# One activation-table set for the first group's decays and norms, in a kernel that TensorE bounds later on

## The chip, the cores and the metric

One core of one Trainium2 chip. The metric is the device time of one launch in microseconds (us). A run is compared with runs of the kernel before on the same chip in the same job. The program uses one core, and each run also lists the mean clock that was granted to TensorE. In the profiles PE is TensorE (matmuls), ACT is ScalarE (functions such as Exp), DVE is VectorE, POOL is GpSimd, and SP is SyncE, which issues nearly all of the loads here. A half clock means that the granted clock is 0.50.

## The reference, cut to what matters

Four sequences of 5824 tokens with 256 channels go through a gated recurrence; its result goes through two up-projections (256 to 1024), their product, and two more matrices that the kernel folds into one (1024 to 256).

```python
sig_r = 1.0 / (1.0 + np.exp(-r_gate))
sig_i = 1.0 / (1.0 + np.exp(-i_gate))
log_a = c * sig_r * np.log(np.clip(a_base, 1e-06, 1.0 - 1e-06))[None, None, :]
a_t = np.exp(log_a)                                    # decay
norm = np.sqrt(np.maximum(1.0 - a_t * a_t, 1e-06))     # norm
x_gated = norm * sig_i * x
h = a_t[:, t] * h + x_gated[:, t]                      # for each t
...
a = x @ w1; b = x @ w2
h = a * b @ w3
return (h @ w_out).astype(np.float32)
```

## The kernel before

The tokens are cut into 46 chunks, and the chunks into 17 groups. In Python, a small model of the engines gives each job a time, and the jobs are emitted in the order of these times, so each engine's program order is fixed. Between some of ACT's functions the traces show a table load, an instruction of its own (1283 ns in the mean in before). A job carries a `kind`: the table set that the model thinks it needs (0: tanh and exp, 1: square root, 2: exp and log). Only group 0 (chunks 0 to 2) makes its norm with Ln and Exp; the other groups use Sqrt.

```python
def decay(c, cb):
    ...
    nc.scalar.activation(out=a, in_=pr, func=AF.Exp, scale=la4[:, cb:cb + 1], bias=la4[:, cb:cb + 1])

def root(c):
    w = sizes[c]
    if any(c in g for g in groups[:N_LOG]):            # N_LOG = 1
        n = T["n", c][:, :, :w]
        nc.scalar.activation(out=n, in_=n, func=AF.Ln, scale=-1.0, bias=1.0)
        nc.scalar.activation(out=n, in_=n, func=AF.Exp, scale=0.5)
        return
    ...                                                # Sqrt

def up(c, mp, nm, w_sb):                               # the up-projections on PE
    pp = psum.tile([P, 2, CT], F32, name=nm, tag="pab")
    for _ in range(warm.get((nm, c, mp), 0)):          # warming matmuls, overwritten afterwards
        nc.tensor.matmul(out=pp[:, 0, :P], lhsT=ident, rhs=ident, start=True, stop=True)
    ...

def rates():
    nc.scalar.preload_act_table_set("natural_log_exp_and_others")
    nc.scalar.activation(out=la4, in_=la4, func=AF.Exp, scale=-1.0)
    nc.scalar.activation(out=la4, in_=la4, func=AF.Ln, bias=1.0)
    ...

# ... the model gives `order`; w3 comes in eight pieces, loaded through two buffers (wf),
# cast by DVE (w_t), transposed by PE (ptw), copied by DVE (w3t), multiplied by PE (pw)
for _, _, key in sorted(order):
    if jobs[key]["fn"]:
        jobs[key]["fn"]()
```

Of the kernel before, what the change touches and what calls it, by code (L numbers as in the profile page):

```python
# [20 lines left out]
def kernel(  # L21
# [12 lines left out]
    nc = tc.nc  # L34
# [47 lines left out]
    T = {}  # L82
# [8 lines left out]
    DV_COPY = set()  # L91
# [214 lines left out]
    def copy_to(dve, dst, src_ps):  # L306
        if dve:
            nc.vector.tensor_copy(out=dst, in_=src_ps)
        else:
            nc.scalar.copy(out=dst, in_=src_ps)  # L310

    def copy(c, mp):
        w = sizes[c]
        sa = ffn.tile([P, 2, CT], BF16, name="sa", tag="sa")
        copy_to(mp == 0 and c in DV_COPY, sa[:, :, :w], T["pa", c, mp][:, :, :w])
        T["sa", c, mp] = sa

    def product(c, mp):
# [84 lines left out]
        nc.vector.tensor_copy(out=ident, in_=ident_f)  # L403

    def rates():
        nc.scalar.preload_act_table_set("natural_log_exp_and_others")
        nc.scalar.activation(out=la4, in_=la4, func=AF.Exp, scale=-1.0)
        nc.scalar.activation(out=la4, in_=la4, func=AF.Ln, bias=1.0)
        nc.vector.tensor_scalar(la4, la4, -1.0, LN_LO, op0=ALU.mult, op1=ALU.max)
        nc.vector.tensor_scalar(la4, la4, LN_HI, 4.0, op0=ALU.min, op1=ALU.mult)  # L410
# [10 lines left out]
    jobs = {}  # L421
# [4 lines left out]
    def job(key, eng, occ, lat, due, fn, after=(), new=None, uses=(), dma=0.0, kind=None, lock=0):  # L426
        due += OFFSET.get(key[0], 0.0) + SHIFT.get(key[:2], 0.0)
        jobs[key] = dict(eng=eng, occ=occ, lat=lat, due=due, fn=fn, after=list(after), new=new, dma=dma, kind=kind,
                         lock=lock, bulk=dma > 0 and key[0] not in ("turn_r", "turn_u", "store", "fold_t"))
        for u in uses:  # L430
            users.setdefault(u, []).append(key)
# [3 lines left out]

    job(("ident",), "DVE", 0.3, 0.35, -1.0, cast_ident)
    job(("la",), "ACT", 0.42, 1.0, 0.0, rates, [("tanh_i", 0)], kind=2)

    def weight(key, piece, dst, due, new=None):
# [33 lines left out]
    for k, g in enumerate(groups):  # L473
        log = k < N_LOG
        for c in g:
# [50 lines left out]
            for mp in range(4):  # L526
                t = U + SLOT / 4 * mp * f
                w = 0.8635 * f * (1.7 if c == 0 else 1)
                job(("pa", c, mp), "PE", w, w + 0.22, t, partial(up, c, mp, "pa", w1_sb),
                    [("cast", c), ("w1", mp // 2)], ("pab", ("pa", c, mp)), [("y", c)])  # L530
                job(("pb", c, mp), "PE", w, w + 0.27, t + 0.01, partial(up, c, mp, "pb", w2_sb),
                    [("pa", c, mp), ("w2", mp // 2)], ("pab", ("pb", c, mp)), [("y", c)])
                e, o, s = ("DVE", 0.065, 1.067) if mp == 0 and c in DV_COPY else ("ACT", 0.05, 0.853)
                job(("copy", c, mp), e, o + s * f, o + s * f + (0.115 if e == "DVE" else 0.15), t + 0.9, partial(copy, c, mp),
                    [("pa", c, mp)], ("sa", ("sa", c, mp)), [("pa", c, mp)])
                job(("product", c, mp), "DVE", 0.065 + 1.067 * f, 0.18 + 1.067 * f, t + 2.0, partial(product, c, mp),
                    [("copy", c, mp), ("pb", c, mp)] + ([("product", c, mp - 1)] if mp else []),
                    None if mp else ("g", ("g", c)), [("sa", c, mp), ("pb", c, mp)])
            for j in range(sizes[c] // P):
# [5 lines left out]
                if c == len(sizes) - 1:  # L545
                    e, o, l = ("ACT", 0.265, 0.42) if j % 2 else ("DVE", 0.332, 0.467)
# [4 lines left out]
                elif j % 2:  # L551
                    e, o, l = ("DVE", 0.599, 0.734) if c in DV_EVAC else ("ACT", 0.48, 0.63)
# [21 lines left out]
    def startable(key, t):  # L574
        b = jobs[key]
        for d in b["after"]:
            if d not in done:
                return False
            if (done[d][0] if jobs[d]["eng"] == b["eng"] and not jobs[d]["dma"] else done[d][1]) > t:
                return False  # L580
        if b["new"]:
            pool = b["new"][0]
            if len(taken[pool]) >= BUFS[pool]:
                for u in users[taken[pool][-BUFS[pool]]]:
                    if u not in done or done[u][1] > t:
                        return False
        if b["lock"] and port_free > t:
            return False
        if b["kind"] is not None and in_run is not None and run_of.get(key) != in_run:
            return False  # L590
        return not b["bulk"] or dma_free <= t + BACKLOG

    events = [0.7, 0.75]
    while any(waiting.values()):
# [3 lines left out]
        for e in engines:  # L598
            if free[e] > t:
                continue  # L600
            key = next((k for k in waiting[e][:80] if startable(k, t)), None)
# [33 lines left out]

    nc.scalar.dma_start(out=la4, in_=a_param.rearrange("(cb p) -> p cb", p=P))

    for _, _, key in sorted(order):
        if jobs[key]["fn"]:
            jobs[key]["fn"]()  # L640
# [1 line left out]
_INS = ['x', 'r_gate', 'i_gate', 'a_param', 'moe_w1', 'moe_w2', 'moe_w3', 'moe_w_out']  # L642
_OUTS = [((23296, 256), 'float32')]
# [25 lines left out]
```

## Time and profile before

| | before |
|---|---|
| time, the first three runs | 532.75 to 534.76 us, median 534.08 |
| the profiled run | 531.5 us (span of the core 529.7), mean granted clock 0.997 |
| busy: PE, ACT, DVE, POOL | 94%, 89%, 84%, 65% of the span |
| table loads | 38, each 1283 ns |

The busy shares are an average over a start of some 70 us, in which nearly every engine waits for another in turn, and a long stretch in which PE is full. The prediction below shows the stages.

### The profile page before, as it was taken

The page shows a single profiled execution, that of the slowest core. Times are in us where ns is not written, and L with a number is a line of the kernel's source. Part 1 is how long each engine was busy: PE and PEld are TensorE (multiplying, and loading weights), DVE is VectorE, ACT ScalarE, POOL GpSimd, SP SyncE. Part 2 cuts the span into 40 slices and gives each one's busy share as a digit, 9 for nine tenths or more (in the row PEclk, how much of TensorE's full clock was granted, in tenths as well). Part 3 has the DMA queues.
Part 4 walks back from the last instruction along what each step waited for, and adds up shares of the span by engine and source line. Part 5 has one row for each costly group of instructions (what it writes and reads, how often), then busy time and mean ns, then how long its engine had stood idle before and what let it go on. Part 6 is the DMA issues. An engine that isn't in the chain of part 4 may idle for free.

```text
span 529.7 us, 8819 instructions
## 1 busy us (share of the span) xinstructions
PE 499.7 (94%) x3199; PEld 308.1 (58%) x3199; DVE 445.0 (84%) x373; ACT 473.4 (89%) x556; POOL 343.6 (65%) x266
## 2 busy tenths in 40 slices
PE   1569889999999999999999999999999999999997
PEld 0456566555666565656656566665556566556556
DVE  0679987999988888988899988989988889899842
ACT  6999999999899998989989999899989999995552
POOL 3347787577758666788675787787685757875100
PEclk9989999999999999999999999999999999999999
DMA  8999959999998999999599797979999988534113
GB/s 304 399 340 325 303 161 263 323 261 267 324 285 209 266 245 265 237 217 274 160 276 278 201 281 178 277 203 252 260 262 237 268 238 244 125 81 101 40 54 106
DMA packets 178828, 124.32 MB, mean 235 GB/s; under 512 B 88672, under 2 KB 174432, under 8 KB 178784
## 3 DMA queue, kind: packets, MB, share of 16 engines
q1 hardware_dynamic: 178512, 123.76, 85.3%
q8 instruction: 25, 0.41, 0.3%
q14 instruction: 19, 0.16, 0.1%
q10 hardware_dynamic: 272, 0.00, 0.0%
HBM read 78.91 MB, written 23.86 MB: 194 GB/s over the span
## 4 chain that ended last, share of the span: by engine, by line
PE 82%; DVE 6%; DMA 4%; ACT 4%; issue 2%; POOL 1%; DVEq 0%; ACTq 0%; POOLq 0%
PE po L333 27%; PE pa L302 27%; PE pb L302 27%; DVE g_t L322 2%; DVE h_t L283 2%; DMA r_t<-in_r_gate_dram 2%; DMA rt<-th_r 1%; DMA ut<-u_t 1%; DVE nrm L268 1%; PE pw L398 1%; ACT L255 1%; POOL u_t L212 1%; DMA la<-in_a_param_dram 1%; ACT a_t L241 1%; DVE w_t L370 1%
## 5 line engine op out<-in xcount | busy, mean ns | idle before, releaser
L322 DVE TENSOR_TENSOR g_t<-sa,pb 128x1024 bf16<-128x1024 bf16 (+1 forms) x184 | 219.0, 1199 | 54.3 <-ACT sa L310 39.2
L302 PEld LDWEIGHTS <-w_sb 128*128 128x128 bf16 x1472 | 143.9, 98 | 143.6 <-issue 3.5
L310 ACT CAST sa<-pa 128x1024 bf16<-128x1024 f32 (+1 forms) x184 | 183.0, 998 | 28.5 <-PE pa L302 26.7
L302 PE MATMUL pb<-y_t,w_sb 128*128 128x512 bf16 (+1 forms) x736 | 187.8, 378 | 1.5 <-DVE g_t L322 1.2
L302 PE MATMUL pa<-y_t,w_sb 128*128 128x512 bf16 (+1 forms) x736 | 187.5, 377 | 0.9 <-DVE g_t L322 0.9
L333 PE MATMUL po<-wp_sb,g_t 128*128 128x256 bf16 x1456 | 180.7, 273 | 0.5 <-ACT wp_sb L414 0.5
L333 PEld LDWEIGHTS <-g_t 128*128 128x128 bf16 x1456 | 142.5, 98 | 45.3 <-issue 0.6
L283 DVE TENSOR_TENSOR_SCAN h_t<-a_t,h_t,nrm 128x512 f32<-128x512 f32 (+3 forms) x90 | 135.0, 1509 | 1.8
L248 POOL TENSOR_TENSOR nrm<-a_t 128x512 f32<-128x512 f32 x80 | 97.4, 1231 | 45.0 <-ACT a_t L241 42.3
L212 POOL TENSOR_TENSOR u_t<-th_i,x_t 128x512 bf16<-128x512 f32 x80 | 121.3, 1532 | 5.0 <-issue 2.8
L291 POOL CAST y_t<-h_t 128x1024 bf16<-128x1024 f32 (+1 forms) x42 | 48.6, 1158 | 68.7 <-DVE h_t L283 57.5
L196 POOL TENSOR_SCALAR th_i<-th_i 128x1024 f32<-128x1024 f32 x44 | 59.5, 1353 | 26.3 <-ACT th_i L191 26.3
L310 ACT COPY ot<-po 128x512 f32<-128x512 f32 (+1 forms) x91 | 53.0, 583 | 17.5 <-PE po L333 16.1
L241 ACT ACTIVATE a_t<-rt,la 128x512 f32<-128x512 bf16 x80 | 63.4, 816 | 2.0 <-DMA rt<-th_r 1.9
L268 DVE SCALAR_TENSOR_TENSOR nrm<-nrm,ut 128x1024 f32<-128x1024 f32 x40 | 60.8, 1521 | 1.6 <-ACT nrm L257 1.1
L191 ACT ACTIVATE th_i<-i_t 128x1024 f32<-128x1024 f32 (+1 forms) x46 | 48.4, 1054 | 2.3 <-DMA i_t<-in_i_gate_dram 2.2
L257 ACT ACTIVATE nrm<-nrm 128x1024 f32<-128x1024 f32 x43 | 44.9, 1063 | 0.2
L184 ACT ACTIVATE th_r<-r_t 128x1024 bf16<-128x1024 f32 x40 | 42.3, 1065 | 0.0
L220 PE MATMUL ptr<-ident,th_r 128*128 128x128 bf16 x44 | 4.5, 260 | 17.0 <-ACT th_r L182 15.7
L257 ACT ACT_TABLE_LOAD x15 | 19.2, 1283 | 0.3
L248 DVE TENSOR_TENSOR nrm<-a_t 128x512 f32<-128x512 f32 (+1 forms) x12 | 12.1, 1053 | 6.4 <-ACT a_t L241 6.4
L220 PEld LDWEIGHTS <-th_r 128*128 128x128 bf16 x44 | 3.5, 116 | 17.9 <-ACT th_r L182 16.9
(39 smaller groups left out, 148.8 us busy)
## 6 DMA issues: line engine op xcount, KB each, us to landing
i_t<-in_i_gate_dram SPq DMA_DIRECT2D x45, 512.0 KB, 5.4
x_t<-in_x_dram SPq DMA_DIRECT2D x45, 512.0 KB, 4.8
r_t<-in_r_gate_dram SPq DMA_DIRECT2D x45, 512.0 KB, 5.4
out_dram<-ot SPq DMA_DIRECT2D x89, 256.0 KB, 3.6
wf<-in_moe_w_dram SPq DMA_DIRECT2D x12, 512.0 KB, 5.2
wf<-in_moe_w_out_dram SPq DMA_DIRECT2D x2, 512.0 KB, 6.9
rt<-th_r SPq DMA_TRANSPOSE x40, 4.9
ut<-u_t SPq DMA_TRANSPOSE x40, 4.8
```

Of the source, the lines that this page charges most:

```text
L196: nc.gpsimd.tensor_scalar(t, t, 1.0, 1.0, op0=ALU.add, op1=ALU.mult)
L212: nc.gpsimd.tensor_mul(out=u.rearrange("p cb j q -> p j cb q")[:, js], in0=cut(t)[:, js], in1=cut(T["x", c])[:, js])
L241: nc.scalar.activation(out=a, in_=pr, func=AF.Exp, scale=la4[:, cb:cb + 1], bias=la4[:, cb:cb + 1])
L248: eng.tensor_mul(out=T["n", c][:, cb, :w], in0=T["a", c][:, cb, :w], in1=T["a", c][:, cb, :w])
L257: nc.scalar.activation(out=T["n", c][:, :, :w], in_=T["n", c][:, :, :w], func=AF.Sqrt, scale=-1.0, bias=1.0)
L268: nc.vector.scalar_tensor_tensor(out=T["n", c][:, :, :w], in0=T["n", c][:, :, :w], scalar=1e-3, in1=T["pu", c][:, :, :w], op0=ALU.max, op1 ...
L283: nc.vector.tensor_tensor_scan(T["h", c][:, cb, lo:hi], T["a", c][:, cb, lo:hi], T["n", c][:, cb, lo:hi], init, ALU.mult, ALU.add)
L291: eng.tensor_copy(out=T["y", c][:, :, :w], in_=T["h", c][:, :, :w])
L302: nc.tensor.matmul(out=pp[:, q, :w], lhsT=w_sb[:, cb, m * P:(m + 1) * P], rhs=T["y", c][:, cb, :w], start=(cb == 0), stop=(cb == NCB - 1))
L310: nc.scalar.copy(out=dst, in_=src_ps)
L322: nc.vector.tensor_mul(out=T["g", c][:, 2 * mp:2 * mp + 2, :w], in0=T["sa", c, mp][:, :, :w], in1=T["pb", c, mp][:, :, :w])
L333: nc.tensor.matmul(out=po, lhsT=T["g", c][:, k, j * P:(j + 1) * P], rhs=wp_sb[:, k, :], start=(k == 0), stop=(k == KD - 1), skip_group_che ...
```

## The change

The intent: have one table set active from the first decay of group 0 to its last norm, where the compiler had put in a load in front of every Ln and every Exp (six loads, the first at 17.25 us, the last at 28.24, 1.28 us each).

```diff
@@ rates
-        nc.scalar.preload_act_table_set("natural_log_exp_and_others")
         nc.scalar.activation(out=la4, in_=la4, func=AF.Exp, scale=-1.0)
@@ end of the program
+    table = None
     for _, _, key in sorted(order):
-        if jobs[key]["fn"]:
-            jobs[key]["fn"]()
+        kind = jobs[key]["kind"]
+        if kind == 2 and table != 2:
+            nc.scalar.preload_act_table_set("natural_log_exp_and_others")
+        if kind is not None:
+            table = kind
+        jobs[key]["fn"]()
```

Two lines more turn `mp == 0 and c in DV_COPY` into `(c, mp) in DV_COPY`; the set is empty in both, so they change nothing.

More of the change, by code (lines that the diff above doesn't have):

```diff
@@ L314, in copy @@
         sa = ffn.tile([P, 2, CT], BF16, name="sa", tag="sa")
-        copy_to(mp == 0 and c in DV_COPY, sa[:, :, :w], T["pa", c, mp][:, :, :w])
+        copy_to((c, mp) in DV_COPY, sa[:, :, :w], T["pa", c, mp][:, :, :w])
         T["sa", c, mp] = sa
@@ L532 @@
                     [("pa", c, mp), ("w2", mp // 2)], ("pab", ("pb", c, mp)), [("y", c)])
-                e, o, s = ("DVE", 0.065, 1.067) if mp == 0 and c in DV_COPY else ("ACT", 0.05, 0.853)
+                e, o, s = ("DVE", 0.065, 1.067) if (c, mp) in DV_COPY else ("ACT", 0.05, 0.853)
                 job(("copy", c, mp), e, o + s * f, o + s * f + (0.115 if e == "DVE" else 0.15), t + 0.9, partial(copy, c, mp),
```

## The prediction

> **What bounds the kernel now.** I first read the table by stage (busy microseconds of each engine in each stretch; the columns after the length are PE, PEld, DVE, ACT, POOL, then granted PE clock, DMA share, GB/s).
>
> ```profile
> 0.00:20.00 20.00, 4.25 (x32) 3.23 (x32) 6.93 (x11) 15.94 (x20) 6.39 (x11) 1.00 0.91 336
> 20.00:31.50 11.50, 5.64 (x58) 5.25 (x58) 6.47 (x10) 11.37 (x12) 5.74 (x6) 1.00 1.05 391
> 31.50:34.80 3.30, 3.21 (x28) 2.83 (x29) 2.77 (x4) 3.29 (x6) 0.84 (x1) 0.60 0.68 218
> 34.80:50.00 15.20, 15.18 (x117) 9.52 (x116) 13.81 (x17) 14.44 (x18) 11.50 (x9) 0.97 1.09 354
> 50.00:72.60 22.60, 19.57 (x163) 13.26 (x161) 20.03 (x22) 21.87 (x29) 15.11 (x13) 1.00 0.79 257
> 72.60:527.00 454.40, 451.87 (x2808) 273.98 (x2805) 395.01 (x312) 406.48 (x476) 304.05 (x229) 1.00 0.85 222
> ```
>
> From 72.6 us to the end PE is busy 451.87 of 454.40 us. There the matmuls set the time, and only 2.5 us of idle PE can be had. So a change in the start is worth exactly what it moves the moment at which PE is filled for good (about 72.6 us). In 20 to 31.5 us ACT is busy 11.37 of 11.50 us and PE half of it, and the DMA engines are full (share 1.05, 391 GB/s). What ACT does there stands in its timeline (start, length):
>
> ```profile
> 12.59 1.06 ACT L182 ACTIVATE th_r<-r_t 128x1024 bf16<-128x1024 f32 x1 [0.31 <-DMA r_t<-in_r_gate_dram]
> 13.55 3.68 ACT L241 ACTIVATE a_t<-ptr,la 128x256 f32<-128x256 bf16 x6
> 17.25 1.28 ACT L254 ACT_TABLE_LOAD   x1
> 18.54 0.63 ACT L254 ACTIVATE nrm<-nrm 128x512 f32<-128x512 f32 x1
> 19.19 1.28 ACT L255 ACT_TABLE_LOAD   x1
> 20.48 0.63 ACT L255 ACTIVATE nrm<-nrm 128x512 f32<-128x512 f32 x1
> ...
> 28.24 1.28 ACT L255 ACT_TABLE_LOAD   x1
> 29.53 1.06 ACT L255 ACTIVATE nrm<-nrm 128x1024 f32<-128x1024 f32 x1
> 30.50 1.04 ACT L182 ACTIVATE th_r<-r_t 128x1024 bf16<-128x1024 f32 x1
> ```
>
> The three norms of the first group are Ln and then Exp, and each of the six gets a table load of its own. The chain of waits runs through all of them. The tanh of chunk 3 at 30.50 comes behind them, and two things hang on it: PE's next transpose, which PE meets in its program order, and the r load that reuses the buffer, at which SP stands with all loads behind it. First PE's timeline, then SP's, then two lines of DVE's:
>
> ```profile
> 26.99 0.60 PE L302 MATMUL pa<-y_t,w_sb 128*128 128x256 bf16 x4
> 31.59 0.62 PE L220 MATMUL ptr<-ident,th_r 128*128 128x128 bf16 x8 [4.00 <-ACT th_r L182]
> ```
> ```profile
> 24.55 0.50 SPq L173 DMA_DIRECT2D i_t<-in_i_gate_dram  x1
> 31.56 0.38 SPq L173 DMA_DIRECT2D r_t<-in_r_gate_dram  x1
> 32.05 0.46 SPq L357 DMA_DIRECT2D wf<-in_moe_w_dram  x1
> ```
> ```profile
> 37.84 0.69 DVE L370 CAST w_t<-wf 128x1024 bf16<-128x1024 f32 x1
> 39.76 1.22 DVE L322 TENSOR_TENSOR g_t<-sa,pb 128x1024 bf16<-128x1024 bf16 x1 [0.63 <-ACT sa L310]
> ```
>
> PE waits 4.00 us, SP issues nothing for 7.0 us, and the first w3 piece, issued at 32.05, lands 4.4 us later by the view of DMA issues of that moment, at about 36.5. DVE casts it at 37.84. From 36 to 70 us DVE waits only 1.4 us in all (three waits for sa in its table of waits), so from there to the first output matmuls it is DVE, with the folding of w3, that paces PE.
>
> [...] the rates (L407 Exp, L408 Ln) run 0.24 us apart behind one preload at 4.98 us with no load between, and the tanh after them gets a load at 6.73. [...] The trace has 1283 ns for each load, but the Ln at 18.54 ends at 19.17, the load runs 19.19 to 20.47 and the Exp starts at 20.48[...], so I count 1.29 us each. [...] after the gap of 4.00 us the granted clock is 0.60 in 31.50 to 34.80 and 0.97 in the next stretch.
>
> **The change part by part.** The edits of the copy (the set of copies that go to DVE is empty) and of the test for a job without a function change no instruction. The times that order the program are computed as before, so I expect the same order on every engine.
> - *The rates' preload* moves from the function to the loop over the jobs; it stays directly ahead of the rates. Zero.
> - *Removed*: the six loads of 17.25 to 29.52, 6 x 1.29 = 7.7 us.
> - *Added*: one load ahead of the six decays (they are now Exp of the same set as the norm), and one ahead of the tanh at 30.50, which today finds its set loaded by the last Exp: 2 x 1.29 = 2.6 us. Two Exp-to-Ln borders may also overlap by some 0.1 us each again, as other neighbours do.
> - *ACT's sum*: decays start at 14.95 and end at 18.6 (today 17.23, +1.3); Ln and Exp of chunk 0 end at 19.9 (21.11, -1.3); those of chunks 1 and 2 at about 21.9 (25.86) and 24.0 (30.59); a load to 25.3; tanh of chunk 3 from 25.3 to 26.3 (31.54). **ACT is 5.2 us ahead** at that point: (6-2) x 1.29.
>
> Now what comes of it. *PE*: its first up-projection is not moved much: the cast of y of chunk 0 stands on POOL behind a weight cast that ends at 24.09 because of its DMA, and 38 warming matmuls come ahead. It begins at about 25.5 to 26 instead of 26.12. The third matmul group ends at 26.5 to 27.5, the tanh is ready by then, and the 4.00 us wait goes, and with it the half clock, which today costs about 1.4 us more (4+12+4 matmuls of 31.6 to 34.8 at twice their time, half of some 2.8 us). At this point PE is 4.5 to 5 us ahead.
>
> *DVE*: scans, products and the third scan move forward by 3 to 4.7 us, as the norms arrive earlier and DVE has 1.24, 2.80 and 1.08 us of idle time ahead of those three. It would want to cast the first w3 piece at about 33.2.
>
> *DMA*: here I expect the gain to be cut. SP issues the r load at 26.4 instead of 31.56, but the 16 engines are full until nearly 32 us. Only the hole after that closes: the bandwidth in 31.5 to 34.8 is 218 GB/s against 391 before it, so (1 - 218/391) x 3.3 = 1.5 us of transfer time is idle. The w3 piece can then land at about 36.5 - 1.4 = 35.1. DVE stands before it for nearly 2 us, and casts at 35.1, which is 2.7 us earlier than today instead of 4.7. The next waits for sa after it (0.63 and 0.28 us today) can be absorbed, up to 0.9 us: 2.7 + 0.4 = **3.1 us**, with 2.7 to 3.6 as its bounds. The later w3 pieces need the queue to stay full to keep this up; I estimate it just can (eleven transfers at 1.3 to 1.5 us until the fifth piece make it land at about 50.2, where DVE would want it at 50.5 or so).
>
> From 72.6 us on PE is the bound and its work is unchanged, so the lead stays: 534.1 - 3.1 = **531.0 us**.
>
> **Rivals.** (a) *The whole of ACT's gain arrives*: 5.2 us, even a little more with the warm clock, so 528.5 to 529. For it: PE's wait is for ACT and is 4.00 us, and the DMA queue has its own hole there. Against it: the full DMA queue and the w3 piece that DVE meets in program order. (b) *DMA eats nearly all*: the weights and inputs of the first 60 us arrive at their own pace (the share is 1.05 to 1.09 in 20 to 31.5 and 34.8 to 50 us), and the wait for ACT becomes waits for w3, w_out and input loads: 1 us or less of gain, 533 to 534. For it: the shares. Against it: DVE shows no wait for a DMA at all in 36 to 70 us, many loads wait for buffers that now come free earlier, and the GB/s falls to 257 in 50 to 72.6, so there is room. (c) *The tanh set comes back or the compiler puts its own loads in spite of the preload*: the gain would be 0 or a loss of 1.3 us, 534 to 535.5. Against it: the same preload ahead of the rates suppresses such loads today. (d) *Given back later*: a smaller lead of the loads over the matmuls brings new PE waits after 72.6. Against it: that stretch has 2.5 us of PE idle time, and DMA is not full there (share 0.85).
>
> **Range and chances.** My weights: 60% for the cut gain (530.2 to 531.8), 20% for (a), 15% for (b), 5% for (c) and (d). The three runs of before spread over 2.0 us, so I widen by 0.7 on each side: 529.0 to 533.0. Two per cent is 10.7 us, twice what ACT saves, so within 2% is nearly sure.
>
> **What would show it.** In the profile after: one load in front of the first decay and none between the Ln and Exp, a load in front of the tanh of chunk 3, four loads fewer in all; that tanh at about 25.3; PE's 4.00 us wait gone and no half clock at 31 to 35 us; r issued at about 26.4; a wait of DVE of 1 to 2 us for the first w3 piece at about 35; PE full from about 69.5. Should DVE not wait for w3 and PE be full before 68.5, (a) is right; should several waits for DMA stand in DVE's, ACT's or POOL's rows in 30 to 70 us, (b). A time above 533 with the loads gone would prove my reading of the start wrong.

The 1.29 us of a load are the 1283 ns of the trace and the gap to its neighbour; the 1.3 to 1.5 us of a transfer are an estimate, 512 KB at the 391 and 354 GB/s of the stage table. That the half clock goes when PE's wait goes rests on the one trace.

## The result, and the profile after

The kernel after ran 531.07 us in the median of 4 runs (530.77 to 531.54), before 534.22 in the median of 4 (532.75 to 534.76). The ratio is 0.9946, with a 95% interval of 0.9925 to 0.9967; the interval leaves out 1. Here and below a ratio is the mean time of one kernel's fast runs over that of the other's in the same rounds, so it is not quite the ratio of the medians quoted. The number was forecast nearly to the tenth. The two traces do not tell that story: their spans are 529.7 and 529.3 us.

The stages of the kernel after, with the columns that the prediction explains:

```profile
20.00:31.50 11.50, 9.37 (x106) 8.82 (x107) 11.50 (x15) 10.93 (x14) 6.04 (x5) 1.00 1.05 389
31.50:34.80 3.30, 1.97 (x15) 1.06 (x14) 1.95 (x3) 2.65 (x4) 2.57 (x3) 1.00 1.06 373
34.80:50.00 15.20, 11.69 (x85) 6.56 (x84) 13.57 (x14) 10.93 (x13) 10.04 (x8) 1.00 1.13 331
```

Between 20 and 31.5 us PE has 9.37 us of work done where it had 5.64, and from 31.5 us on the clock is full. (Before about 25 us the clock column cannot be trusted: eight transposes take 1.04 us at 21.57 and 0.61 us at 26.98.) But from 34.8 to 50 us PE is busy 11.69 us where it was busy 15.18: the lead is lost there. ACT did what was asked (its timeline, start and length):

```profile
13.50 1.28 ACT L641 ACT_TABLE_LOAD   x1
14.79 3.70 ACT L241 ACTIVATE a_t<-ptr,la 128x256 f32<-128x256 bf16 x6
18.36 0.65 ACT L254 ACTIVATE nrm<-nrm 128x512 f32<-128x512 f32 x1
19.04 0.63 ACT L255 ACTIVATE nrm<-nrm 128x512 f32<-128x512 f32 x1
...
23.76 1.28 ACT L182 ACT_TABLE_LOAD   x1
25.05 1.06 ACT L182 ACTIVATE th_r<-r_t 128x1024 bf16<-128x1024 f32 x1
```

One load ahead of the decays, none between Ln and Exp, and the tanh of chunk 3 at 25.05 instead of 30.50: 5.45 us earlier. PE's transpose of it follows its neighbour at once (PE's timeline; the wait of 4.00 us is gone):

```profile
26.54 0.60 PE L302 MATMUL pa<-y_t,w_sb 128*128 128x256 bf16 x4
26.98 0.61 PE L220 MATMUL ptr<-ident,th_r 128*128 128x128 bf16 x8
```

Now the SP timeline of after, and below it DVE's. The two lines after those are the view of DMA issues narrowed to the issue of the first w3 piece, in before (32.05) and in after (29.32); their last column is the time to landing.

```profile
26.14 0.38 SPq L173 DMA_DIRECT2D r_t<-in_r_gate_dram  x1
29.32 0.33 SPq L357 DMA_DIRECT2D wf<-in_moe_w_dram  x1
```
```profile
36.29 1.31 DVE L370 CAST w_t<-wf 128x1024 bf16<-128x1024 f32 x1 [2.84 <-DMA wf<-in_moe_w_dram]
38.97 1.21 DVE L322 TENSOR_TENSOR g_t<-sa,pb 128x1024 bf16<-128x1024 bf16 x1
```
```profile
wf<-in_moe_w_dram SPq DMA_DIRECT2D x1, 512.0 KB, 4.4
```
```profile
wf<-in_moe_w_dram SPq DMA_DIRECT2D x1, 512.0 KB, 6.9
```

The piece was issued 2.7 us earlier and landed at 36.2 instead of 36.5. By its landing the DMA engines had moved 13.05 MB since the start, in before 12.58 MB: the time of the former hole in the queue went to other transfers, and the views do not say to which. DVE, which was 4.46 us ahead one instruction before (its product at 32.77, before at 37.24), waits 2.84 us for it. It is 1.55 us ahead at the cast and 0.79 us at the next product, since cast and square now take 1.31 and 1.52 us where they took 0.69 and 0.68. POOL is at work beside them this time (a square from 36.02, then its pass over th_i until 38.51; in before it is idle from 37.29 to 38.91). In the two traces the casts of w3 on DVE take 0.67 to 0.69 us where POOL is idle and 0.69 to 1.69 us where it works beside them. That POOL is the cause is not shown: no run here takes it away.

What is left at the first output matmul, from which PE is full, in before and in after:

```profile
70.60 3.65 PE L333 MATMUL po<-wp_sb,g_t 128*128 128x256 bf16 x32 [0.47 <-ACT wp_sb L414]
```
```profile
70.24 3.65 PE L333 MATMUL po<-wp_sb,g_t 128*128 128x256 bf16 x32 [0.47 <-ACT wp_sb L413]
```

Of a lead of 5.45 us on ACT 0.36 us arrive, and the timed runs differ by 3.1 us. The experiments are about this gap.

### The profile page after: what moved, and what is told of

It is laid out like the page before. It is cut to its first block, busy times and chain, and to the rows that moved or that the text cites. A ratio compares the mean times of both kernels' runs of the same rounds, so it can differ in the third digit from the quotient of the medians.

```text
span 529.3 us, 8760 instructions
## 1 busy us (share of the span) xinstructions
PE 495.5 (94%) x3144; PEld 306.8 (58%) x3199; DVE 446.9 (84%) x373; ACT 469.2 (89%) x552; POOL 344.3 (65%) x266
## 4 chain that ended last, share of the span: by engine, by line
PE 83%; DVE 7%; issue 3%; DMA 2%; POOL 2%; ACT 2%; DVEq 0%; POOLq 0%; ACTq 0%
PE po L333 28%; PE pa L302 27%; PE pb L302 27%; DVE g_t L322 2%; DVE h_t L283 2%; DMA r_t<-in_r_gate_dram 2%; POOL u_t L210 1%; DVE nrm L268 1%; DVE w_t L370 1%; DVE nrm L265 1%; ACT a_t L241 1%; DMA la<-in_a_param_dram 1%; PE pw L398 1%; POOL th_i L196 0%; DVE w3t L393 0%
## 5 line engine op out<-in xcount | busy, mean ns | idle before, releaser
L302 PE MATMUL pb<-y_t,w_sb 128*128 128x512 bf16 (+1 forms) x718 | 184.9, 377 | 2.4 <-DVE g_t L322 1.2
L302 PE MATMUL pa<-y_t,w_sb 128*128 128x512 bf16 (+1 forms) x699 | 183.1, 377 | 3.5 <-POOL u_t L210 0.9
L257 ACT ACT_TABLE_LOAD x15 | 19.2, 1283 | 0.3
## 6 DMA issues: line engine op xcount, KB each, us to landing
i_t<-in_i_gate_dram SPq DMA_DIRECT2D x45, 512.0 KB, 5.1
x_t<-in_x_dram SPq DMA_DIRECT2D x45, 512.0 KB, 4.7
r_t<-in_r_gate_dram SPq DMA_DIRECT2D x45, 512.0 KB, 5.3
wf<-in_moe_w_dram SPq DMA_DIRECT2D x12, 512.0 KB, 5.6
wf<-in_moe_w_out_dram SPq DMA_DIRECT2D x2, 512.0 KB, 7.3
```

What stands on the lines that cost most here:

```text
L257: nc.scalar.activation(out=T["n", c][:, :, :w], in_=T["n", c][:, :, :w], func=AF.Sqrt, scale=-1.0, bias=1.0)
L302: nc.tensor.matmul(out=pp[:, q, :w], lhsT=w_sb[:, cb, m * P:(m + 1) * P], rhs=T["y", c][:, cb, :w], start=(cb == 0), stop=(cb == NCB - 1))
```

## The experiments

Twelve kernels ran in three jobs, each on its own chip, every one in five rounds (6 runs; 11 of before in each job). Theory A: what costs time in before is PE's wait of 4.00 us together with the half clock that follows it, in some executions for longer than in the trace at hand. Theory B: the chain as a whole is 3 us ahead in each run, as predicted.

The first job gave before 532.89 us in the median (532.23 to 537.49), the second 533.62 (532.41 to 534.88), the third 533.95 (532.65 to 535.59).

### e0: before again

No edit.

> The kernel before, unchanged, under another name, for the spread of its executions and a second trace. The two traces at hand differ by only 0.36 us at the first output matmul (70.60 before, 70.24 after) and 0.4 us in the span, although the timed runs differ by 3.1 us. Theory A (a clock theory): PE's wait of 4.00 us for the tanh of chunk 3 halves PE's clock for a time that differs from run to run; the trace of before caught a short one. Then the spans here range from about 529.7 to 533 with the granted mean clock falling as the span grows (0.997 at 529.7; about 0.99 at 533), and a second trace in a slower run shows its first output matmul later than 70.6 us. Theory B (the lead of the prediction is there in each run): clocks are all about 0.997 and a second trace shows the first output matmul about 3 us after that of the kernel after. Ratio to before 1.000 either way.

533.66 us (532.46 to 537.17), ratio 1.0014 [0.9976, 1.0052]. The clocks do differ from run to run: 1.0 (532.46 us), 0.997 (532.58 and 532.65), 0.994 (534.66 and 536.32), 0.99 (537.17). In the trace of before the clock is 0.50 from 32.15 to 35.56 us. One such stretch of 3.4 us takes 0.5 x 3.4/531 = 0.0032 from the mean, so by this estimate these are no, one, two and three stretches. The kept trace is the run of 532.58; it has one (0.67 in 31.5 to 34.8 us, 0.96 in 34.8 to 50), and its first output matmul is at 71.53. So the trace of before with which I started was at the favourable end: executions of the same program differ by 0.9 us in the start and by up to two more stretches of half clock, which it didn't have.

### e1: before, with PE's wait filled

```diff
+    warm["pa", 0, 1] = 58
```

> The kernel before with 58 more warming matmuls ahead of the third up-projection group of chunk 0, so that PE is busy in most of its 4.00 us wait; ACT keeps all its table loads. Theory A: no half clock at 31 to 35 us, mean clock 1.000, and most of the gain of the change is had without the change: 531 to 532 us, with a spread under 1 us. Theory B: the tanh still comes at 30.5, so 534 us as before, at the best 0.5 us less.

531.12 us (530.65 to 536.05), ratio 0.9978 [0.9938, 1.0018]: four runs at 530.65 to 531.23, all at clock 1.0, and two at 534.58 (0.996) and 536.05 (0.997). PE's timeline:

```profile
27.04 3.40 PE L298 MATMUL pa<-ident 128*128 128x128 bf16 x58
30.27 0.60 PE L302 MATMUL pa<-y_t,w_sb 128*128 128x256 bf16 x4
31.32 0.62 PE L220 MATMUL ptr<-ident,th_r 128*128 128x128 bf16 x8 [0.45 <-ACT th_r L182]
...
69.84 3.33 PE L333 MATMUL po<-wp_sb,g_t 128*128 128x256 bf16 x29 [0.47 <-ACT wp_sb L414]
```

ACT has all its table loads and its tanh comes as late as in before. PE's wait is down from 4.00 to 0.45 us, and the half clock is gone (1.00 instead of 0.60 in 31.5 to 34.8 us); the third group itself comes 3.3 us later (30.27 instead of 26.99), behind the warming matmuls. The first output matmul is at 69.84, earlier than in any trace of before or after. So in its four clear runs this kernel is where after is, without the change. The mean of the six is not clearly better than before, because of the two runs with a half clock, which have no trace; e3 below shows a place where it can come.

### e2: after, first two w3 pieces ahead in the queue

```diff
+    ahead(("load", "w3", 0), ("i", 5))    # moves one job in the order to just before another
+    ahead(("load", "w3", 1), ("x", 6))
```

> The kernel after with two load issues moved forward on SP: the first w3 piece ahead of the i load of chunk 5, the second ahead of the x load of chunk 6. Nothing else moves. If the queue's order of transfers is what cut the lead (my prediction's DMA step; the trace of after has DVE waiting 2.84 us for that piece), the piece lands at about 33.5 instead of 36.27, DVE's wait falls below 0.5 us, the first output matmul comes 1.5 to 2.7 us earlier than in the trace of after (70.24), and the time is 528.5 to 529.8 us. If the lead is lost in DVE's own work behind it, or the later pieces set the pace, the wait goes away or moves to a later piece and the time stays at 530.5 to 531.5.

A miss: 534.01 us (532.14 to 536.19), ratio 1.0007 [0.9971, 1.0042], so after's gain is lost, and not to the half clock: the three runs at clock 1.0 are at 533.87 to 534.76. The first piece is there in time (DVE casts it at 35.55 without a wait), but SP stands at the moved issues, DMA moves 356 instead of 389 GB/s in 20 to 31.5 us, and DVE now waits for later pieces:

```profile
46.77 1.08 DVE L370 CAST w_t<-wf 128x1024 bf16<-128x1024 f32 x1 [1.22 <-DMA wf<-in_moe_w_dram]
...
56.23 0.69 DVE L370 CAST w_t<-wf 128x1024 bf16<-128x1024 f32 x1 [2.52 <-DMA wf<-in_moe_w_dram]
```

The first output matmul comes at 73.44.

### e3: after, with the load ahead of the norms only

```diff
-        if kind == 2 and table != 2:
+        if kind == 2 and table != 2 and key[0] != "decay":
...
-            table = kind
+            table = 0 if key[0] == "decay" else kind
```

> The kernel after with the added load in front of the first norm instead of in front of the decays: the decays use the tanh's set again, as in before. As many table loads as in after. If only the number of loads before the tanh of chunk 3 counts, the time is that of after, 531.1 within 0.5 us; the six decays come 1.29 us earlier, the tanh at the same 25.05. If it helps that squares and scans start earlier, up to 0.5 us less.

531.37 us (530.41 to 534.05), ratio 0.9968 [0.9936, 1.0001]. Four runs at clock 1.0 are at 530.41 to 531.37, as after; two with a half clock are at 533.21 and 534.05. Where the load stands in the group does not matter in what these runs can tell. Its trace happens to be the run of 533.21 and shows where a half clock can come late: the first output matmul is at 69.49, but then PE waits 2.37 us at 117.56 and runs at half clock for the next 3.4 us. The second fence is the stage table of this stretch and of the one before it:

```profile
117.56 1.02 PE L302 MATMUL pb<-y_t,w_sb 128*128 128x512 bf16 x4 [2.37 <-DVE g_t L322]
```
```profile
115.17:118.59 3.42, 1.05 (x7) 0.54 (x6) 3.42 (x3) 1.49 (x3) 3.34 (x3) 1.00 1.08 373
118.59:122.00 3.41, 3.41 (x13) 1.71 (x12) 2.45 (x3) 1.06 (x3) 1.27 (x2) 0.50 1.12 283
```

### f0: after again

No edit.

> The kernel after, unchanged, beside more runs of before on one chip. Theory A (PE's long wait and its half clock are the cost; the saved time of ACT beyond that wait is worth little): most runs have a mean clock of 1.000 and 531.0 to 531.5 us, as in the kernel before with its wait filled with warming matmuls (531.12); a run with a half clock elsewhere reaches 533 to 536; before has a clock of 0.997 or lower in nearly each run, 532.3 to 532.8 with one window of half clock and about 534.5 or more with two. Theory B (a lead of 3 us of the whole chain): before with a mean clock of 0.997 is 3 us longer than after with 1.000.

532.16 us (530.82 to 532.83) beside 533.62 of before; ratio 0.997 [0.9952, 0.9988]. That is 1.5 us in the medians, not 3.1. All six clocks are 0.999 or 1.0. The runs fall into two kinds, 530.82 and 530.95, and 532.08 to 532.83. The kept trace is of the upper kind (532.25) and starts as the first trace of after did (first output matmul at 70.27), but PE waits 2.37 us at 118 where the first trace waits 0.78. PE's lines of this place, first trace and f0:

```profile
117.33 0.81 PE L302 MATMUL pb<-y_t,w_sb 128*128 128x512 bf16 x3 [0.78 <-DVE g_t L322]
```
```profile
118.33 1.02 PE L302 MATMUL pb<-y_t,w_sb 128*128 128x512 bf16 x4 [2.37 <-DVE g_t L322]
```

So PE can be held up once more, 45 us after it is full, by an amount that varies between executions.

### f1 and h1: after, with two needless loads

```diff
+        if key == ("tanh_r", 3):
+            nc.scalar.preload_act_table_set("exp_and_others")
+            nc.scalar.preload_act_table_set("natural_log_exp_and_others")
```

> The kernel after with two needless table loads put in front of the tanh of chunk 3, so that half of the time saved on ACT is lost again: the tanh at about 27.6 instead of 25.05, a wait of PE for it of 1.3 us. Theory A with the DMA queue as the limit (the first w3 piece lands at 36.3 whenever the tanh comes within some 3 us): the first output matmul within 0.5 us of after's 70.24, clock 1.000, time 531.0 to 531.7. Theory B: 2.6 us later than after, 533.5.

531.04 us (530.45 to 531.32), ratio 0.9952 [0.9937, 0.9967]; first output matmul at 69.90. On another chip the same kernel, expected as follows, was run again:

> The kernel after with two needless loads again: on one chip it ran 531.04 against 532.16 of after itself. If that is real (the delay moves the transfers so that PE's wait at 118 us stays at 0.8 us), its runs are all at 530.4 to 531.4 again and after has some at 532 and more. If it was chance, both kernels show both kinds. In either case the 2.6 us of ACT that the two loads cost are not to be seen.

It gave 531.31 us (530.71 to 531.74), ratio 0.9949 [0.9932, 0.9966], beside h0 at 531.48; first output matmul at 70.36. None of its twelve runs has a half clock, and none is over 531.74. ACT's tanh of chunk 3 comes at 28.42 in f1's trace, after three loads in a row; DVE then waits less for the same w3 piece:

```profile
27.12 1.28 ACT L182 ACT_TABLE_LOAD   x1
28.42 1.06 ACT L182 ACTIVATE th_r<-r_t 128x1024 bf16<-128x1024 f32 x1
```
```profile
36.71 1.22 DVE L370 CAST w_t<-wf 128x1024 bf16<-128x1024 f32 x1 [1.04 <-DMA wf<-in_moe_w_dram]
```

This is the sharpest result: 2.6 us of ACT's gain given away cost nothing. Whether the kernel is even a little better than after can't be said: it was 1.1 us ahead of f0 and 0.2 us ahead of h0.

### f2: after, with four needless loads

The edit of f1, with the pair of loads twice.

> The kernel after with four needless loads there: ACT does as many loads as in before, the tanh at about 30.2, PE's wait about 3.7 us. Theory A: the half clock is back in most runs (0.997 or lower) and the time is that of before on this chip, 532.3 to 534.5. Theory B: 5.2 us later than after, or at the most before's time. The step from two to four loads tells: under A nearly all of the loss is in it, under B it is as large as the step from none to two.

532.58 us (531.67 to 534.51), ratio 0.9989 [0.9969, 1.0008], so no longer to be told from before, and 1.5 us above f1 on the same chip. Three of the six runs have a half clock (0.996, 0.997, 0.994). The loss is in the second pair of loads and not in the first, as theory A has it. It is not the half clock alone: the three runs at clock 1.0 (531.67 to 532.61, mean 532.2) are 1.2 us above f1's mean too, and what they lose was not found. The kept trace (531.67) is one without a half clock, though PE waits 3.51 us, and its first output matmul is at 70.50; the second fence is the stage after the wait:

```profile
31.88 0.62 PE L220 MATMUL ptr<-ident,th_r 128*128 128x128 bf16 x8 [3.51 <-ACT th_r L182]
```
```profile
31.50:34.80 3.30, 2.92 (x36) 2.70 (x37) 2.43 (x3) 3.30 (x6) 1.04 (x1) 1.00 0.65 212
```

The length of a wait does not tell in these traces whether a half clock follows. It follows the 4.00 us in before (0.50 from 32.15 to 35.56 us) and the 2.37 us in e3 (0.50 from 118.59 to 122.00). It does not follow the 2.37 us in f0 (1.00 in 118.6 to 122 us) or the 3.51 us in f2 (1.00 in 31.5 to 34.8, as above). What else decides was not tested.

### f3: after, with one load moved back in the queue

```diff
+    ahead(("i", 5), ("i", 6))
```

> The kernel after with one load moved back on SP: i of chunk 5 (which ACT uses only at about 57 us) is issued just ahead of i of chunk 6 instead of in front of r of chunk 6 and the first w3 piece. No issue is held up by it. If the queue of transfers cuts the lead, the first w3 piece lands 1.3 to 1.5 us earlier (about 34.8 instead of 36.27), DVE's wait for it shrinks from 2.84 to about 1.4 us, the first output matmul comes about 0.7 to 1.5 us before after's 70.24, and the time is about 530 us with clock 1.000. If another thing behind it is the limit, the time stays at 531.

A miss in the time: 532.86 us (530.38 to 536.33), ratio 0.9996 [0.9965, 1.0026], with two runs at a lower clock (0.99 and 0.997). The trace (the run of 536.33) shows that the first piece did come earlier, by 1.1 us (landed at 35.15; 1.3 to 1.5 us were expected), and what became of it. DVE's casts of the first and the fifth w3 piece:

```profile
35.17 1.57 DVE L370 CAST w_t<-wf 128x1024 bf16<-128x1024 f32 x1
...
53.47 0.69 DVE L370 CAST w_t<-wf 128x1024 bf16<-128x1024 f32 x1 [1.54 <-DMA wf<-in_moe_w_dram]
```

The wait of 2.84 us ahead of the first piece is gone, DVE is 1.1 to 1.7 us ahead of after until 45 us, and then 1.54 us go into a wait for the fifth piece; the first output matmul comes at 71.47. With e2 this says that the order of the queue moves the wait from one piece to another and doesn't take it away.

### g0 and g1: a failed edit, and so two more repeats; h0: after once more

The w3 pieces were to be loaded by half, in before (g0) and in after (g1), to take bytes from the queue:

```diff
+        if key[1] == "w3":
+            nc.sync.dma_start(out=T[key].rearrange("p a b -> p (a b)")[:, :512], in_=piece[:, 0, :512])
+            return
```

> Wrong result on purpose. The kernel before, with each of the eight w3 pieces loaded by half (256 KB instead of 512 KB, the other half of the buffer is stale), which takes some 0.65 us of each transfer out of the queue. Control for the next run. In the trace of before DVE waits for no w3 piece, so the first output matmul should come at most 0.5 us earlier than in a run of before, and the time should be 531.5 to 533, the half clock at 31 to 35 us included.

> Wrong result on purpose. The kernel after with the same halved w3 loads. If the queue of transfers is what eats ACT's lead, the first piece lands at about 35 and the later ones 0.65 us earlier with each piece, DVE's wait for the first piece falls from 2.84 to about 1.4 us, the first output matmul comes 1.5 to 3 us earlier than in after (67.2 to 68.7 instead of 70.24), and the gain over the control is 2.5 to 3.5 us at that point. If DVE's own work from 36 to 70 us is what eats it, the first output matmul stays within 0.7 us of 70.24.

> The kernel after a third time, for its spread on another chip and as the neighbour of the next run. So far its runs fall into 530.8 to 531.5 and 532.1 to 532.8 us; the trace of the upper kind has PE waiting 2.4 instead of 0.8 us at about 118 us. Both kinds again; ratio to before 0.995 to 0.998.

The 0.65 us for half a piece, in the first two of these texts, is an estimate: 256 KB at the 391 GB/s that before shows in 20 to 31.5 us are 0.67 us.

The condition was wrong: the name is in `key[0]`, so the branch is never taken. The results were correct, which a halved w3 could not give, and g1's view of DMA issues still has 512.0 KB for each piece. So g0 is before and g1 is after once more, and whether fewer bytes in the queue would let the lead through stays open. As repeats they are of use: g0 532.88 us (531.66 to 537.28), ratio 0.9988 [0.9958, 1.0018], first output matmul at 71.34; g1 532.12 (530.94 to 532.89), ratio 0.9962 [0.9945, 0.9979], 70.69. h0, after a third time: 531.48 (530.57 to 533.12), ratio 0.9954 [0.9936, 0.9973], 70.63; all clocks 1.0, and one run at 533.12. With the runs of g1 and h0 between 531.4 and 532.1 the two kinds of f0 are no longer apart.

### All runs of before and of after together

Stretches of half clock per run are estimated from its mean clock as in e0. Before: the 33 runs of the three jobs, e0 and g0. After: its first 4 runs, f0, g1 and h0.

| stretches of half clock | before: runs, mean us | after: runs, mean us |
|---|---|---|
| none | 5, 532.3 | 22, 531.7 |
| one | 30, 533.4 | 0 |
| two | 9, 535.5 | 0 |
| three | 1, 537.2 | 0 |
| all | 45, 533.8 | 22, 531.7 |

The difference of the means is 2.1 us (by the ratios beside before of the same job: 2.9 for the first comparison, 1.6 for f0, 2.0 for g1, 2.5 for h0). Among runs without a half clock 0.6 us are left (of before only five runs). So about 1.5 us go with the half clock, which 40 of 45 runs of before have and no run of after. This is a sorting of runs, on several chips, and not yet a proof of cause.

The start gives another division, which can't be added to the first. The first output matmul is at 70.60, 71.53 and 71.34 in the three traces of before (mean 71.16) and at 70.24, 70.27, 70.69 and 70.63 in the four of after (mean 70.46), 0.7 us apart. In before and e0 the half clock lies ahead of that point (0.60 and 0.67 in 31.5 to 34.8 us), and g0's run, at 0.997, has one stretch by the estimate; so these 0.7 us include it. In e1 and f2, where ACT's tanh is as late as in before (30.77 us in f2, 30.50 in before) but the clock in 31.5 to 34.8 us is 1.00, it is at 69.84 and 70.50, as early as in after. So in the traces ACT's lead brings nothing at this point that the absence of the half clock does not bring.

The other 1.4 us lie in runs without a trace: the traced runs of before took 531.5, 532.58 and 533.06 us, and the mean of the 45 is 533.8. Ten of the 45 have more than one stretch of half clock. Those with one go from 532.2 to 535.8, so the number of stretches is not all that counts. From the first output matmul to the end e3, with its half clock at 118.59 us, takes 461.9 us, f3, whose mean clock is 0.997, 463.1, and the other twelve traces 459.0 to 460.2. That runs of before lose their time at 118 us too is a guess, and not shown.

## Why the prediction was right or wrong

- **The loads and ACT: right.** Four loads fewer (38 to 34 in the groups of ACT's instructions), none between Ln and Exp, the tanh at 25.05 (forecast 25.3), each load 1.28 us. In before the six Ln and Exp had got six loads, although the rates' Exp and Ln (6.27 and 6.51 us) had run behind one preload of the set (4.98 us), with no load between; with the preload ahead of the decays they got none.
- **PE's wait and the half clock after it: right** that both go. I added the half clock to PE's lead in the start and gave it no weight of its own in the sum, with one trace as the whole evidence. Sorted by it, the runs put 1.5 of 2.1 us with it. e1 speaks for it as a cause: with PE's wait filled and ACT as late as before, four of six runs are as fast as after, though the mean of the six is not clearly better than before. f1 and f2 speak for it from the other side, f2 only in part.
- **DMA cuts the lead: right in kind, too weak in size. This is the step that failed.** I let the w3 piece land 1.4 us earlier because a hole in the queue would close. The hole did close (373 instead of 218 GB/s in 31.5 to 34.8 us), but other transfers got its time, the piece landed only 0.2 us earlier, and the rate in the stage behind fell from 354 to 331 GB/s. DVE cast at 36.29, not at 35.1. Two longer instructions on DVE took half of the rest (1.55 us of lead fell to 0.79). Hence 0.4 us at the first output matmul in the first pair of traces and 0.7 in the means, the half clock's part included, where I had 3.1. Rival (b) was the better account of the start.
- **"The lead stays" from 72.6 us: not quite.** PE is held up once more at about 118 us, by 0.8 or by 2.4 us, in one and the same program. A longer wait, as rival (d) has it, thus turns up in some executions (f0 and e3, 2.37 us each) and not in the first pair of traces (0.77 us in before, 0.78 in after); whether before has it in runs without a trace is not shown.
- **Rivals (a) and (c): false.** ACT's further 2.6 us are worth nothing (f1, h1), and the preload was obeyed.
- **The number** of 531.0 us held by luck, because two errors met. The lead at the first output matmul was put 2.4 us too high (3.1 for 0.7), and what the runs of before lose beyond the start, some 1.4 us, was left out. The rest is the draw: before's first four runs had a mean of 534.0, its 45 later ones 533.8; after's first four had 531.1, all 22 have 531.7. That is how 3.1 us in the first comparison and 2.1 us over all go together. The range has a slip of its own: 530.2 to 531.8 widened by 0.7 on each side is 529.5 to 532.5, not 529.0 to 533.0. The measured time lies in both.

**What stays open.** No trace caught a run of before with two stretches of half clock, so where the second one lies is not shown; e3 has one at 118.59 us after a PE wait of 2.37 us. Why a wait of 2.37 us is followed by a half clock in e3 and by none in f0 is not shown either. Which transfers took the time of the closed hole was not looked up by transfer. Why the wait at 118 us has two sizes was not tested. The halved loads have to be tried with a correct edit. No version tried clearly beats after.

## What to carry to other kernels

Before pricing an engine's saved time, find the first thing that its followers need which it does not itself produce. Here it is a w3 piece from a full DMA queue (share 1.05 to 1.13 from 20 to 50 us in after), and reordering the queue only moved the wait (e2, f3). Where a trace shows a half clock behind a TensorE wait, price it too, and from many executions, since here a wait of 2.37 us was followed by one in e3 and by none in f0: one trace is one draw, and if the profiled run is faster than every timed run, something that costs time is missing from the trace. Cheap tests that pay: give the saved time back in steps (none, half, all), and fill the bound engine's wait without touching what it waits for.
